# Clustered attention and a softplus layer on one core: weight steps with one VectorE operation fewer, an upright first pass, keys 4 to 7 held back, a shorter softplus

## The chip, the cores and the metric

The kernel runs on one core of one Trainium2 chip. Such a core has five engines that run side by side and meet at semaphores: TensorE (PE, matrix products; its weight loads are listed as PEld), VectorE (DVE), ScalarE (ACT), GpSimd (POOL) and SyncE (SP, which here only issues transfers). Each takes its instructions in the order in which they were written for it. Sixteen DMA engines carry the transfers that SP and ACT issue. Products accumulate in PSUM, everything else lies in SBUF.

The metric is the device time of one execution in microseconds; before the change it is 899.57 us, the median of three runs.

## What is computed

Attention of 4 batches with 8 heads over 768 positions of 64 numbers, in which a query sees only the keys of its own cluster, and then a layer with softplus. Cut to what matters:

```python
q_n, k_n, c_n = (x / (norm(x) + 1e-6) for x in (q, k, centroids))   # 16 centroids a head
q_assign = argmax(einsum('bhsd,hcd->bhsc', q_n, c_n), -1)           # and k_assign likewise
mask   = q_assign[:, :, :, None] == k_assign[:, :, None, :]
scores = where(mask, q @ k.T / 8, -1e9)
attn   = exp(scores - max(scores)); attn = attn / (sum(attn) + 1e-9)
x = concat_heads(attn @ v)                                          # 3072 x 512
h = x @ w_in                                                        # 512 -> 2048
g = maximum(h, 0) + log1p(exp(-abs(h)))                             # softplus
out = g @ w_out                                                     # 2048 -> 512
```

The inputs are drawn at random with fixed spreads. The two weight matrices come in as 64-bit floats, the rest as 32-bit floats.

## The kernel before

**Numbers in two halves.** A 32-bit value is carried as two f16 tiles, a rounded one and the rest. A product is then three f16 products (rounded x rounded, and the two mixed ones). The rest is always made on POOL by subtraction (lines 336, 372, 457, 641, 719, 795), after ACT made the rounded half (lines 335, 368, 455, 639, 717, 794).

**Passes.** A pass is half of one batch's query positions: 8 passes, each with 8 heads and 3 query tiles of 128 positions, 24 tiles. Tile `t` of pass 0 is `t < 24`; pass 0 and 1 belong to batch 0.

**Preparation.** `prep_k` loads two heads' keys, splits them, transposes them, lets `nearest` find each key's centroid (small products with `cents`, then a row of small DVE operations), and writes into the second tile `n2` of each key its rounded numbers and, beside them, 16 columns that hold 0 for its own cluster and a large negative number for the others. `prep_q` does the same for four heads' queries and waits for the clusters that have a key at all (`al`, made in `clusters`). So a score with its mask is a sum of two products over 128 rows (lines 574 to 582). `turn` transposes either on PE through PSUM (keys 0 to 7 and the queries of pass 0) or by a DMA transpose in SP's queue (`flip`). `prep_v` loads and splits the values. `prep_weights` has 32 steps, 16 for `w_in` and 16 for `w_out`: a step loads 512 KB of 64-bit floats into a staging room (most rooms are parts of the tile `wo` itself), and rebuilds a 32-bit float from the two words: ACT takes the magnitude of the high word, scaled down so far that the exponent is rebased (line 320), DVE shifts it left by three bits (322), joins the sign bit of the high word (326) and joins three bits of the low word (332). ACT and POOL then make the two f16 halves (335, 336).

**Scores and attend.** For each tile `scores` makes four 384-wide matmuls (line 576) into one of two PSUM banks pairs of the ring `s`, DVE takes the negated maximum of each row (592), ACT the exponential with it as bias (600). From pass 1 on, ACT and POOL split the result (639, 641) and a DMA transpose turns two tiles at once (650) for `attend`, which multiplies by the values (683 to 685; a column of ones gives the sum of the weights). In pass 0 this is done in 32 bits instead: ACT also accumulates the sum (`accum_out`), PE transposes the weights (617, six of 128x128, against a 32-bit unit matrix `eye32`), ACT and DVE copy them out of PSUM (625, 623), and `attend` multiplies with the unsplit values (679). Lines 702 to 710 divide by the sums.

**The layer.** `ffn1` makes 16 tiles of `h` in each pass (752 to 754), `softplus` turns each into two halves of `g`: DVE sets the sign bit (771), ACT takes Exp and Ln(1 + .) (773, 774), DVE adds max(h, 0) (783), then the split (794, 795). `ffn2` sums over 16 of these (817 to 819) into the one PSUM bank of the ring `o`, in two halves of 8, for three output tiles; `store` scales and adds (833, 837) and SP writes the result (840).

**Order.** No engine decides what it does next. When the program is built, the class `Order` runs every piece of work as a generator that yields operations with an engine and an assumed time in ns, and waits on events and on rings of buffers (`ring`). It always emits the operation that can start first by these assumed times; a priority breaks ties only. Operations marked `shared` are planned so that DVE and POOL do not overlap. So an assumed time, a wait or an engine that changes in one place changes the written order of all engines. All loads are issued in ACT's queue (line 221), transposes and stores in SP's. Where the plan leaves PE idle for more than 600 ns, `warm` (line 204) writes small filler matmuls.

Of the kernel before, what the change touches and what calls it, by code (L numbers as in the profile page):

```python
# [17 lines left out]
MASK = 65504.0  # L18
# [7 lines left out]
NPE = 8  # L26

REBASE = 2.0**-112

# [84 lines left out]
def tile_cluster_attention__then__softplus_ffn(  # L114
# [47 lines left out]
    cf = cpool.tile([P, D], F32, name="cf")  # L162
    nc.sync.dma_start(cf, centroids.rearrange("h c d -> (h c) d"))
    tab = cpool.tile([P, 2 * NT, NCL], F16, name="tab")
# [9 lines left out]
    eye32 = p2.tile([P, P], F32, tag="ot", name="eye32", bufs=QT)  # L174
    nc.gpsimd.tensor_copy(eye32, eye)
# [10 lines left out]
    for i in range(2):  # L186
        t = cpool.tile([P, 2 * NT, P], F16, name=f"n2_{i}")
        nc.gpsimd.memset(t[:, :, D + NCL :], 0.0)
        N2.append(t)


    od = Order()

    eye32_key = od.get("ot", QT)[1]
# [25 lines left out]
    def load(dst, src, nbytes):  # L220
        return op("ACT", 60, lambda: nc.scalar.dma_start(dst, src), dma=nbytes / 290.0)
# [10 lines left out]
    def prep_centroids():  # L232
        sq = p2.tile([P, D], F32, tag="x32", name="csq", bufs=1)
# [53 lines left out]
    def prep_weights(step: int):  # L287
# [30 lines left out]
        if f >= 0 and f // 2 in rooms:  # L318
            yield wait("wr", rooms[f // 2])
        yield op("ACT", 630, lambda: nc.scalar.activation(mag, val, AF.Abs, scale=sc))  # L320
# [5 lines left out]
            lambda: nc.vector.scalar_tensor_tensor(high, high, -0x80000000, mab, ALU.bitwise_and, ALU.bitwise_or),  # L326
# [31 lines left out]
    def prep_v(n: int):  # L358

        vk = yield from ring("vb", NP)  # L360
        rk, vf = yield from raw_tile("v", n, [P, 2, NT, D])
        yield load(vf, rows(v, n, 0, NT, 2), P * 2 * NT * D * 4)
        vb = VB[n // 2 % NP]
        raw_v[n] = vf, rk
# [17 lines left out]
    def turn(dst, src, name: str, on_chip: bool):  # L382
# [4 lines left out]
        for g in range(0, dst.shape[1], NT):  # L387
# [8 lines left out]
            if g:  # L396
                yield op("DVE", 950, lambda g=g, ps=ps: nc.vector.tensor_copy(dst[:, g : g + NT], ps))
# [6 lines left out]
    def nearest(xs, heads, low: int, sfx: str, twin: int):  # L404
# [28 lines left out]
        yield op("DVE", 345, lambda: nc.vector.tensor_tensor(sim, sim, tab[:, :nt], ALU.mult))  # L433
# [10 lines left out]
    def prep_k(n: int):  # L444

        kkey[n // 2] = yield from ring("kt", NP)
        rk, kf = yield from raw_tile("k", n, [P, 2, NT, D])
# [27 lines left out]
            250,  # L475
# [8 lines left out]
    def clusters(n, ps, eq, hk):  # L484
# [4 lines left out]
        if h % 4 == 0:  # L489
            alive[n] = p2.tile([P, 4, NCL], F16, tag="al", name=f"al_{n}", bufs=4)  # L490
# [5 lines left out]
        yield op("DVE", 150, lambda: nc.vector.tensor_scalar(al, al, 1.0, None, ALU.min), shared=True)  # L496
        od.set(("al", n))

    def prep_q(n: int, pi: int):
# [4 lines left out]
        yield wait("kn", n + 2)  # L504
# [56 lines left out]
    def scores(t: int):  # L561
# [5 lines left out]
        if t:  # L567
            yield wait("sc", t - 1)
# [346 lines left out]
```

## Time and profile before

| | |
|---|---|
| three runs | 896.24, 899.57 and 903.73 us |
| span of the profiled execution | 899.4 us |
| mean granted clock of TensorE | 0.992 |
| moved by DMA | 136.12 MB, mean 151 GB/s |
| first score matmul | 53.1 us from the start |
| last score matmul of the last pass | 779.6 us |

The profile is of one execution. Its span runs from the first to the last instruction, and is 0.2 us below the median of the runs. Instructions of an engine are grouped by their line in the kernel; a group's row has the engine, the operation, the tiles that it writes and reads, the count, and behind the bar the busy time in us and the mean of one in ns, then the idle time of the engine in front of them with what ended it.

The page's strip of 40 slices of 22.5 us each shows where PE is not full (tenths of a slice) and how that lies against the other engines and the transfers:

```profile
PE   7889998989889999999999999999999999999997
...
DVE  4989997778876656765757666657675655433331
ACT  5667686866757677865858777766787576633330
POOL 5322356787857678866757677675777665512110
PEclk8999999999999999999999999999999999999999
DMA  6323759988896879999696989997888655510000
```

DVE is at nine tenths in the second to sixth slice, POOL fills only from the sixth on, and DMA is at nine tenths of its 16 engines in many slices from the eighth on. PE's strip contains the filler of line 204.

### The profile page before, as it was taken

Reading aid. Unit: us, or ns where it says so; the run is one execution under the profiler, and the core shown is the slowest. Engines: PE = TensorE matmul, PEld = TensorE weight load, DVE = VectorE, ACT = ScalarE, POOL = GpSimd, SP = SyncE. Lnnn points to the kernel's source line nnn. Section 1 sums busy time; section 2 is a strip of 40 time slices with the busy share of each in tenths; the row PEclk is TensorE's granted clock in tenths of the full one; section 3 lists DMA queues with packets and bytes.
Section 4 is the critical chain, followed back from the end, with each engine's and each line's share of the span. In section 5 each row is a group of like instructions: output and inputs, shape, how many; then the busy total and the mean of one; then the engine's idle time right before and its main releaser. Section 6 shows DMA issues by size and latency. Waiting matters only on the chain.

```text
span 899.4 us, 20880 instructions
## 1 busy us (share of the span) xinstructions
PE 859.1 (96%) x8650; PEld 562.1 (62%) x8650; DVE 576.5 (64%) x1060; ACT 588.2 (65%) x904; POOL 528.1 (59%) x353
## 2 busy tenths in 40 slices
PE   7889998989889999999999999999999999999997
PEld 7878876655565666655666665555666565655554
DVE  4989997778876656765757666657675655433331
ACT  5667686866757677865858777766787576633330
POOL 5322356787857678866757677675777665512110
PEclk8999999999999999999999999999999999999999
DMA  6323759988896879999696989997888655510000
GB/s 202 117 89 112 154 150 214 202 194 212 168 190 150 189 151 191 226 201 210 149 198 126 187 166 193 195 220 135 182 182 186 145 119 134 111 30 12 25 0 36
DMA packets 393326, 136.12 MB, mean 151 GB/s; under 512 B 369680, under 2 KB 386064, under 8 KB 393232
## 3 DMA queue, kind: packets, MB, share of 16 engines
q1 hardware_dynamic: 371472, 99.15, 56.2%
q10 hardware_dynamic: 21760, 35.66, 13.4%
q8 instruction: 67, 1.10, 0.5%
q14 instruction: 27, 0.22, 0.1%
HBM read 35.68 MB, written 6.29 MB: 47 GB/s over the span
## 4 chain that ended last, share of the span: by engine, by line
PE 73%; DVE 8%; DMA 8%; ACT 4%; issue 3%; POOL 3%; ACTq 1%; POOLq 0%; DVEq 0%
PE s L576 10%; PE o L817 8%; PE o L819 8%; PE o L818 8%; PE h L752 8%; PE h L754 8%; PE h L753 8%; DMA pt<-phl 8%; PE mbank L679 3%; PE mbank L683 3%; PE mbank L685 3%; PE mbank L684 3%; POOL phl L641 2%; PE pT L617 2%; DVE negm L592 2%
## 5 line engine op out<-in xcount | busy, mean ns | idle before, releaser
L641 POOL TENSOR_TENSOR phl<-p,phl 128x768 f16<-128x768 f32 x168 | 278.3, 1672 | 84.8 <-ACT phl L639 61.2
L592 DVE TENSOR_REDUCE negm<-s 128x1 f32<-128x768 f32 x192 | 182.6, 954 | 51.5 <-PE s L576 48.0
L600 ACT ACTIVATE p<-s,negm 128x768 f32<-128x768 f32 x192 | 172.1, 898 | 65.6 <-DVE negm L592 45.5
L795 POOL TENSOR_TENSOR gh<-fg,gh 128x768 f16<-128x768 f32 x64 | 107.2, 1676 | 135.2 <-ACT gh L794 131.8
L752 PE MATMUL h<-xT,wi 128*128 128x384 f16 x512 | 167.4, 327 | 7.4 <-DVE fg L783 5.4
L754 PE MATMUL h<-xT,wi 128*128 128x384 f16 x512 | 167.8, 328 | 0.0
L753 PE MATMUL h<-xT,wi 128*128 128x384 f16 x512 | 167.6, 327 | 0.0
L576 PE MATMUL s<-kt,qt 128*128 128x384 f16 x768 | 155.5, 325 | 3.7 <-ACT p L600 3.3
L819 PE MATMUL o<-wo,gh 128*128 128x512 f16 x384 | 145.8, 380 | 1.1 <-POOL gh L795 1.1
L817 PE MATMUL o<-wo,gh 128*128 128x512 f16 x384 | 146.0, 380 | 0.7 <-DVE ot L837 0.4
L818 PE MATMUL o<-wo,gh 128*128 128x512 f16 x384 | 145.9, 380 | 0.0
L773 ACT ACTIVATE fa<-fa 128x384 f32<-128x384 f32 x128 | 66.6, 521 | 120.1 <-DVE fa L771 119.2
L639 ACT CAST phl<-p 128x768 f16<-128x768 f32 x168 | 134.3, 827 | 16.3 <-DMA pt<-phl 14.1
L771 DVE TENSOR_SCALAR fa<-h 128x384 int32<-128x384 int32 x128 | 71.0, 555 | 107.7 <-PE h L754 107.4
L683 PE MATMUL mbank<-vb,pt 128*128 128x65 f16 x1008 | 108.5, 192 | 8.2 <-DMA pt<-phl 7.8
L684 PE MATMUL mbank<-vb,pt 128*128 128x64 f16 x1008 | 108.5, 192 | 0.0
L685 PE MATMUL mbank<-vb,pt 128*128 128x65 f16 x1008 | 108.2, 194 | 0.0
L683 PEld LDWEIGHTS <-pt 128*128 128x128 f16 x1008 | 93.4, 98 | 22.9 <-DMA pt<-phl 11.4
L783 DVE SCALAR_TENSOR_TENSOR fg<-h,fa 128x384 f32<-128x384 f32 x128 | 70.5, 552 | 53.5 <-ACT fa L774 51.6
L576 PEld LDWEIGHTS <-qt 128*128 128x128 f16 x768 | 71.6, 98 | 49.4 <-issue 6.2
L684 PEld LDWEIGHTS <-pt 128*128 128x128 f16 x1008 | 92.9, 97 | 11.1
L685 PEld LDWEIGHTS <-pt 128*128 128x128 f16 x1008 | 93.1, 97 | 0.0
(122 smaller groups left out, 1289.9 us busy)
## 6 DMA issues: line engine op xcount, KB each, us to landing
wo<-in_moe_w_in_dram ACTq DMA_DIRECT2D x16, 512.0 KB, 3.7
wo<-in_moe_w_out_dram ACTq DMA_DIRECT2D x14, 512.0 KB, 4.0
rawk<-in_k_dram ACTq DMA_DIRECT2D x16, 384.0 KB, 4.7
rawv<-in_v_dram ACTq DMA_DIRECT2D x16, 384.0 KB, 4.6
rawq<-in_q_dram ACTq DMA_DIRECT2D x16, 384.0 KB, 4.1
out_dram<-ot SPq DMA_DIRECT2D x24, 256.0 KB, 2.6
pt<-phl SPq DMA_TRANSPOSE x84, 5.7
wraw<-in_moe_w_out_dram ACTq DMA_DIRECT2D x2, 512.0 KB, 5.3
```

The source lines that it names most:

```text
L576: nc.tensor.matmul(st[:, j, :SH], qt[:, s, i], kt[:, s, NT // 2 * j : NT // 2 * (j + 1)], start=(s == 0), stop=(s == 1),)
L592: yield op("DVE", 950, lambda: nc.vector.tensor_reduce(negm, st[:, :, :SH], AX.XY, ALU.max, negate=True))
L641: "POOL", 1640, lambda: nc.gpsimd.tensor_tensor(phl[:, u, 1], p32, phl[:, u, 0], ALU.subtract), shared=True
L683: nc.tensor.matmul(av, pt[:, 0, c], vb[:, c, D : 2 * D + 1], start=(c == 0), stop=False)
L684: nc.tensor.matmul(av[:, :D], pt[:, 0, c], vb[:, c, :D], start=False, stop=False)
L685: nc.tensor.matmul(av, pt[:, 1, c], vb[:, c, D : 2 * D + 1], start=False, stop=(c == NT - 1))
L752: nc.tensor.matmul(hp, w[0], x[0], start=(c == 0), stop=False)
L753: nc.tensor.matmul(hp, w[0], x[1], start=False, stop=False)
L754: nc.tensor.matmul(hp, w[1], x[0], start=False, stop=(c == NP - 1))
L817: nc.tensor.matmul(po, g[0], wo[:, f, 0, 0], start=(f == f0), stop=False)
L818: nc.tensor.matmul(po, g[0], wo[:, f, 0, 1], start=False, stop=False)
L819: nc.tensor.matmul(po, g[1], wo[:, f, 0, 0], start=False, stop=(f == f0 + NF // 2 - 1))
```

## The change

- **Weight steps.** Line 320 uses the activation Prelu with a slope of 2^32 for negative numbers instead of the magnitude. A negative number then lands 32 exponent steps higher, which after the shift by three is a set sign bit. The join of the sign (line 326) is gone, and line 332 joins the low word's bits to the shifted word.
- **Loads.** All loads are issued by SP instead of ACT, with an assumed 450 ns instead of 60.
- **Upright first pass.** In pass 0 the scores are made with the keys as rows, so that no transpose of the weights is needed. Two 384-wide matmuls on the second product alone (rounded numbers and mask, 96 of the rows) give an estimate of each query's maximum; DVE negates it and splits it into a coarse and a fine part (two operations on 128x1), PE transposes these, ACT writes them into two rows of the transposed queries, 96 and 97, against constant rows of 2048 and 1 in the keys. Twelve 128-wide matmuls then make the shifted scores upright, and ACT takes the exponential straight into the tile that `attend` reads. `eye32`, the 32-bit transposes, their copies and `accum_out` are gone. A column of ones behind the values of pass 0 gives the sums; these values are loaded in two parts, into rows of 65 numbers. Both `m` and `u`, the two score tiles, come from the ring `s`.
- **Keys 4 to 7.** `prep_k` of heads 4 and 6 waits, in the planner, until the first queries' cluster work is through (`qa`); the first queries no longer wait for the second keys' buffer.
- **Softplus.** g = max(h, min(ln(1 + exp h), 20)): Exp reads PSUM directly, line 771 is gone, line 783 becomes one operation with minimum and maximum.
- **Last half.** The last pass's second half of `ffn2` takes its PSUM from the ring `s`, two tiles, instead of the one of `o`.
- **Assumed times and small things.** A DVE copy in `turn` 560 instead of 950, two small DVE operations 450 and 300 instead of 250 and 150. `tab` is one row, read by broadcast.

```diff
@@ prep_weights
-        yield op("ACT", 630, lambda: nc.scalar.activation(mag, val, AF.Abs, scale=sc))
+        yield op("ACT", 630, lambda: nc.scalar.activation(mag, val, AF.Prelu, scale=sc, alpha=SIGN_UP))
         yield op("DVE", 420, lambda: nc.vector.tensor_scalar(mab, mab, 3, None, ALU.logical_shift_left), shared=True)
         yield op(
             "DVE",
             680,
-            lambda: nc.vector.scalar_tensor_tensor(high, high, -0x80000000, mab, ALU.bitwise_and, ALU.bitwise_or),
-            shared=True,
-        )
-        yield op(
-            "DVE",
-            680,
-            lambda: nc.vector.scalar_tensor_tensor(high, low, 29, high, ALU.logical_shift_right, ALU.bitwise_or),
+            lambda: nc.vector.scalar_tensor_tensor(high, low, 29, mab, ALU.logical_shift_right, ALU.bitwise_or),
             shared=True,
         )
@@ load
-        return op("ACT", 60, lambda: nc.scalar.dma_start(dst, src), dma=nbytes / 290.0)
+        return op("SP", 450, lambda: nc.sync.dma_start(dst, src), dma=nbytes / 290.0)
@@ prep_v
-        rk, vf = yield from raw_tile("v", n, [P, 2, NT, D])
-        yield load(vf, rows(v, n, 0, NT, 2), P * 2 * NT * D * 4)
+        rk, vf1 = yield from raw_tile("v", n, [P, 2, NT, D + (n < H)])
+        vf = vf1[:, :, :, :D]
+        if n < H:
+            yield op("POOL", 150, lambda: nc.gpsimd.memset(vf1[:, :, :, D:], 1.0))
+        parts = 2 if n < H else 1
+        for u in range(0, 2, 2 // parts):
+            yield load(
+                vf[:, u : u + 2 // parts], rows(v, n + u, 0, NT, 2 // parts), P * 2 * NT * D * 4 // parts
+            )
@@ prep_k
         kkey[n // 2] = yield from ring("kt", NP)
+        if n in (4, 6):
+            yield wait("qa", 0)
@@ prep_q
-        yield wait("kn", n + 2)
+        yield wait("kn", n + 2 if n else 0)
@@ upright, for each tile of pass 0
+        def emit():
+            for j in range(2):
+                nc.tensor.matmul(
+                    st[:, j, :SH],
+                    qt[:SHIFT, 1, i],
+                    kt[:SHIFT, 1, NT // 2 * j : NT // 2 * (j + 1)],
+                    start=True,
+                    stop=True,
+                )
+        yield op("PE", 330, emit)
...
+        yield op("DVE", 950, lambda: nc.vector.tensor_reduce(negm, st[:, :, :SH], AX.XY, ALU.max, negate=True))
+        od.set(sk)
...
+        yield op("DVE", 90, lambda: nc.vector.tensor_scalar(top, negm, 1.0 / by, None, ALU.mult))
+        yield op("DVE", 90, lambda: nc.vector.scalar_tensor_tensor(rest, top, -by, negm, ALU.mult, ALU.add))
...
+        yield op("PE", 60, lambda: nc.tensor.transpose(out=ps[:KROWS], in_=mc, identity=eye))
+        yield op("ACT", 250, lambda: nc.scalar.copy(qt[SHIFT:KROWS, 1, i], ps[SHIFT:KROWS]))
...
+        def emit():
+            for c in range(NT):
+                to = up[:, c // (NT // 2), c % (NT // 2) * P : (c % (NT // 2) + 1) * P]
+                nc.tensor.matmul(to, kt[:, 0, c], qt[:, 0, i], start=True, stop=False)
+                nc.tensor.matmul(to, kt[:KROWS, 1, c], qt[:KROWS, 1, i], start=False, stop=True)
+        yield op("PE", 690, emit)
...
+        yield op("ACT", 830, lambda: nc.scalar.activation(dst, up[:, :, :SH], AF.Exp))
@@ scores, pass 0
-                for c in range(NT // 2):
-                        nc.tensor.transpose(out=ps[:, c], in_=p32[:, j, c * P : (c + 1) * P], identity=eye32)
...
-                    yield op("DVE", 550, lambda: nc.vector.tensor_copy(dst, ps))
-                else:
-                    yield op("ACT", 490, lambda: nc.scalar.copy(dst, ps))
+        if pi == 0:
+            yield from upright(t)
+            return
@@ softplus
-            lambda: nc.vector.tensor_scalar(a.bitcast(I32), hp.bitcast(I32), -0x80000000, None, ALU.bitwise_or),
-        yield op("ACT", 520, lambda: nc.scalar.activation(a, a, AF.Exp))
+        yield op("ACT", 500, lambda: nc.scalar.activation(a, hp, AF.Exp))
         yield op("ACT", 520, lambda: nc.scalar.activation(a, a, AF.Ln, bias=1.0))
-            "DVE", 550, lambda: nc.vector.scalar_tensor_tensor(g[:, f % 2], hp, 0.0, a, ALU.max, ALU.add)
+            "DVE", 550, lambda: nc.vector.scalar_tensor_tensor(g[:, f % 2], a, TOP, hp, ALU.min, ALU.max)
@@ ffn2
+        if pi == len(passes) - 1 and half:
+            ok = yield from ring("s", 2)
+            po = ps_s.tile([P, 2, DM], F32, tag="s", name=f"o_{b}_{c0 + i}_{half}")[:, 0]
+        else:
+            ok = yield from ring("o", 1)
+            po = ps_o.tile([P, DM], F32, tag="o", name=f"o_{b}_{c0 + i}_{half}")
```

More of the change, by code (lines that the diff above doesn't have):

```diff
@@ L188, in tile_cluster_attention__then__softplus_ffn @@
         nc.gpsimd.memset(t[:, :, D + NCL :], 0.0)
+        for c, m in zip(range(SHIFT, KROWS), SHIFT_BY):
+            nc.gpsimd.memset(t[:, :, c : c + 1], m)
         N2.append(t)
+    MC = []
+    for i in range(2):
+        t = cpool.tile([P, KROWS], F16, name=f"mc_{i}")
+        nc.gpsimd.memset(t, 0.0)
+        MC.append(t)
     od = Order()
-    eye32_key = od.get("ot", QT)[1]
     mbank = ps_m.tile([P, 512], F32, name="mbank")
@@ L232, in prep_centroids @@
     def prep_centroids():
-        sq = p2.tile([P, D], F32, tag="x32", name="csq", bufs=1)
+        sq = cfs[:, 1]
         small = [cpool.tile([P, 1], F32, name=f"c{nm}") for nm in ("ss", "sg", "nrm", "rn")]
@@ L488, in clusters @@
         yield op("PE", 100, lambda: nc.tensor.matmul(cnt, ones, eq, start=True, stop=True))
-        if h % 4 == 0:
-            alive[n] = p2.tile([P, 4, NCL], F16, tag="al", name=f"al_{n}", bufs=4)
+        if n - h % 4 not in alive:
+            alive[n - h % 4] = p2.tile([P, 4, NCL], F16, tag="al", name=f"al_{n}", bufs=4)
         al = alive[n - h % 4][:, h % 4 : h % 4 + 2]
@@ L567, in scores @@
         if t:
-            yield wait("sc", t - 1)
+            yield wait("scm" if tiles[t - 1][1] == 0 else "sc", t - 1)
+        if pi == 0:
+            yield from upright(t)
+            return
         sk = yield from ring("s", 2)
@@ L594, in scores @@
         p32 = p2.tile([P, 2, SH], F32, tag="p32", name=f"p32_{sfx}", bufs=3)
[L595 to L631 removed]
+        yield op("ACT", 900, lambda: nc.scalar.activation(p32, st[:, :, :SH], AF.Exp, bias=negm))
+        od.set(sk)
         if u == 0:
@@ L678, in emit @@
                 for c in range(NT):
[L679 removed]
+                    nc.tensor.matmul(av, pt[:, c], vf[:, c], start=(c == 0), stop=(c == NT - 1))
                 return
@@ L803, in ffn2 @@
         yield wait("g", pi, NF // 4 * half)
-        ok = yield from ring("o", 1)
-        po = ps_o.tile([P, DM], F32, tag="o", name=f"o_{b}_{c0 + i}_{half}")
+        if pi == len(passes) - 1 and half:
+            ok = yield from ring("s", 2)
+            po = ps_s.tile([P, 2, DM], F32, tag="s", name=f"o_{b}_{c0 + i}_{half}")[:, 0]
+        else:
+            ok = yield from ring("o", 1)
+            po = ps_o.tile([P, DM], F32, tag="o", name=f"o_{b}_{c0 + i}_{half}")
         f0 = NF // 2 * half
```

106 lines of the change are left out of this document (58 added, 48 removed).

## The prediction

> **What bounds the kernel now.** I read the page's head, then the windows view cut at the places where the work changes, then the same windows for line 204 alone, then the grouped instructions and the waits. In the windows view each row is a stretch, its length, and the busy us (and instructions) of PE, PEld, DVE, ACT and POOL, then the granted clock, the DMA share and GB/s.
>
> ```profile
> span 899.4 us, 20880 instructions
> ...
> 0.00:53.20 53.20, 42.83 (x731) 40.77 (x732) 38.48 (x114) 28.73 (x41) 22.75 (x23) 0.94 0.48 155
> 53.20:126.00 72.80, 70.94 (x657) 63.21 (x655) 67.11 (x112) 53.44 (x107) 22.72 (x19) 1.00 0.47 118
> 126.00:140.00 14.00, 11.83 (x172) 9.61 (x172) 12.98 (x22) 10.79 (x16) 8.72 (x7) 1.00 0.88 211
> 140.00:280.00 140.00, 122.45 (x1397) 82.04 (x1395) 106.78 (x184) 97.31 (x150) 100.85 (x67) 0.98 0.92 194
> 280.00:876.00 596.00, 592.77 (x5554) 356.08 (x5555) 347.97 (x625) 396.03 (x591) 371.43 (x239) 1.00 0.72 148
> ```
>
> The same stretches for line 204 alone. Its matmuls are filler that the planner puts into gaps, so they are idle time in disguise.
>
> ```profile
> 0.00:53.20 53.20, 30.27 (x435) 28.01 (x435) 0.94 0.48 155
> 53.20:126.00 72.80, 6.64 (x111) 6.28 (x111) 1.00 0.47 118
> 126.00:280.00 154.00, 25.58 (x422) 23.95 (x422) 0.98 0.91 196
> ```
>
> From 280 to 876 PE is busy 592.8 of 596.0 us: nothing but less PE work shortens that. Real PE work (busy less filler) is 12.6 of 53.2 us before the first scores, 64.3 of 72.8 in pass 0, and 108.7 of 154.0 from 126 to 280. So 40.6 + 8.5 + 45.3 = 94 us stand empty before 280, and a little at the end; all that can be won lies there. Within pass 0 the fullest engine beside PE is DVE, 67.1 of 72.8 us. From 126 to 280 none is full: DVE 119.8 of 154.0, POOL 109.6, DMA share 0.91.
>
> **The parts, and what each costs.** The groups that the change touches (busy us and mean ns of one):
>
> ```profile
> L326 DVE SCALAR_TENSOR_TENSOR wo<-wo 128x512 int32<-128x512 int32 x14 | 14.9, 1066 | 0.0
> L326 DVE SCALAR_TENSOR_TENSOR wraw<-wraw,wo 128x512 int32<-128x512 int32 x2 | 1.4, 680 | 0.0
> L623 DVE COPY ptf<-pT 128x384 f32<-128x384 f32 x24 | 13.1, 552 | 0.7 <-PE pT L617 0.2
> L702 DVE TENSOR_SCALAR rs<-mbank 128x6 f32<-128x6 f32 x28 | 4.5, 162 | 13.3 <-PE mbank L685 13.2
> L702 DVE TENSOR_SCALAR rs<-sum 128x6 f32<-128x6 f32 x4 | 2.4, 602 | 0.0
> L625 ACT COPY ptf<-pT 128x384 f32<-128x384 f32 x24 | 11.3, 477 | 5.1 <-PE pT L617 4.7
> L600 ACT ACTIVATION_READ_ACCUMULATOR p<-s,negm 128x1 f32 x24 | 4.7, 195 | 0.0
> ...
> 0.00:53.20 53.20, 4.41 (x5) 0.94 0.48 155
> 53.20:126.00 72.80, 12.28 (x14) 1.00 0.47 118
> 126.00:280.00 154.00, 14.06 (x13) 0.98 0.91 196
> ...
> 126.00:280.00 154.00, 12.15 (x22) 0.98 0.91 196
> ```
>
> The last four rows are windows: DVE time of line 326 in three stretches, then of line 771.
>
> *Weight steps.* Line 326 goes, 19 times before 126. As measured that is 4.41 + 12.28 = 16.7 us of DVE. But an undisturbed one takes 680 ns, and the 1066 of the others is the same operation kept waiting. I count only 0.68, so 19 x 0.68 = 12.9 us. The Trainium skill (GPSIMD Engine Reference, Specifications) says that GpSimd shares its SBUF interfaces with VectorE, and that this hurts DVE instructions with two SBUF inputs or in a two-port mode. By that rule the wait passes to the next such operation and 12.9 us is right; without it the whole 16.7 would go. The spread of 680 to 1066 agrees with the rule.
>
> *Upright pass 0, DVE.* 24 copies of line 623 go: 13.1 us. 48 tiny operations on 128x1 come in. No row is that small; the nearest is line 702 with 128x6, 162 ns from PSUM and 602 from SBUF. 48 x 0.162 = 7.8 us, 48 x 0.602 = 28.9 us. The new ones read SBUF, but POOL, whose work goes with the long ones, is busy only 22.7 of 72.8 us here: 0.162 + 0.31 x 0.44 = 0.30 each, so 14.4 us. Line 702 reads PSUM alone in the changed kernel, four times; that is too little to count. DVE's work until 126 falls by 12.9 + 13.1 - 14.4 = 11.6 us (18.2 with tiny operations at 162 ns, 2.9 more than before at 602).
>
> *Upright pass 0, PE and ACT.*
>
> ```profile
> 60.44 0.66 PE pT L617 x6
> 61.10 1.30 PE s L576 x8
> ...
> 63.06 1.29 PE mbank L679 x12
> ...
> 52.95 0.28 PE qT L393 x5
> ```
>
> A tile now takes 0.65 (four 384-wide score matmuls) + 0.66 (six transposes) + 1.29 us. Changed: 0.33 for the two matmuls of the maximum, about 0.1 for one small transpose, and twelve 128-wide matmuls. These take 0.65 us by columns (0.163 x 128/384 x 12) and 0.98 by the worst nearby row, qT at 0.08 each with its waits; I take 0.68, since they follow each other like the scores. That is 1.11 for 1.31, 5 us less over 24 tiles (between -6 and +2). One more column in line 679 adds 1.29/64, or 0.5 us over pass 0. ACT loses 11.3 + 4.7 us and gains 24 small copies, at most L625's 0.48 each. Both are covered by DVE, which paces the stage.
>
> *Keys 4 to 7 held.* Nothing is removed; two key chains move from before the first scores into pass 0, so scores start well before 53.2. The wait is one of the planner, so no engine stands at it; only the written order changes. I count nothing for it: pass 0 is paced by DVE, whose sum is the same. It is what lets the 11.6 us come out at the end of pass 0. Otherwise PE, with 64.3 - 5 us of work after a start at 53.2, would be next. The cover is the 12 tiles before head 4, some 36 us at 72.8/24; if a chain is late by more, PE waits a few us.
>
> *Loads on SP.* All 80 loads move behind the DMA transposes of SP's queue.
>
> ```profile
> L221 ACTq DMA_DIRECT2D wo<-in_moe_w_out_dram x14: 333/336/486, 105.0 to 245.1; - x14
> 6.50 0.20 ACT L244 ACTIVATE cnrm<-csg 128x1 f32<-128x1 f32 x1 [4.48 <-issue]
> wo<-in_moe_w_out_dram ACTq DMA_DIRECT2D x14, 512.0 KB, 4.0
> ...
> 7.74 1.64 POOL L457 TENSOR_TENSOR kn<-rawk,kn 128x768 f16<-128x768 f32 x1 [5.05 <-ACT kn L455]
> ```
>
> ACT gets back 0.34 us for each, hidden beside PE. At the start the centroids' Ln waits 4.48 us behind the engine's own issues; freed, it moves up by some 2.5 us, and the centroid transposes that PE has in front of the first key's move too. I take 2 us (0 to 2.5). The values' loads are split into rows of 256 bytes and so slower, covered because values are not needed until the first attend. POOL's few new memsets at the start (columns of the value tiles, of N2, the MC tiles) fall into the 5.05 us in which it waits for its first key, up to 7.74; behind that they would cost their own length.
>
> *Shorter softplus.* Line 771 goes, 128 times. 106 of them lie after 280, beside a full PE, and are worth nothing. In the ramp the two removals take 22 x 0.55 = 12.2 us and 14.1 us from DVE. PE's idle time there, by the waits:
>
> ```profile
> PE mbank L683 <- DMA pt<-phl: 5.6, 4, 3.3
> PE h L752 <- DVE fg L783: 5.4, 4, 4.1
> PE mbank L204 <- DVE x L710: 3.3, 2, 1.8
> ```
>
> The DVE-bound ones are 5.4 + 3.3 = 8.7 us, the filler stands for more. Between 0 (DMA sets the ramp) and the whole 26.2 us, I take 7, near the waits that name DVE.
>
> *Second output bank in the last half.*
>
> ```profile
> 883.30 0.23 PE o L819
> 883.56 0.70 DVE ot L837
> 884.30 0.38 PE o L817
> ...
> 877.51 0.56 DVE L771 TENSOR_SCALAR fa<-h 128x384 int32<-128x384 int32 x1 [2.21 <-PE h L754]
> ```
>
> Between two output tiles PE waits from 883.36, when the last matmul's slot ends, to 884.30: 0.94 us, twice, gone with two banks. The last softplus chain before them is shorter by line 771's 0.56. Together 2.4 us.
>
> The corrected due times (250 to 450, 950 to 560) change only the written order; no row prices that, and it is left at nothing.
>
> **Sum.** 899.4 - 11.6 - 2 - 7 - 2.4 = 876.4. The profiled execution's 899.4 is within 0.2 us of the median 899.57, so the sum stands for the median too.
>
> **Rivals.**
> *The ramp closes (about 850).* The tiny operations cost 162 ns, so DVE loses 18 us in pass 0, and all 26.2 us of the ramp come out: 899.4 - 18.2 - 2 - 26.2 - 2.4 = 850.6. For it: DVE at 119.8 of 154. Against: POOL and DMA are as full.
>
> *Loads delay transposes (about 892).* The chain between 126 and 280 has four long waits on a transpose:
>
> ```profile
> 144.08 11.40 DMA pt<-phl
> ...
> 247.58 9.26 DMA pt<-phl
> ...
> 261.11 6.08 DMA pt<-phl
> ...
> 273.09 6.79 DMA pt<-phl
> ```
>
> A weight load takes 4.0 us to land. If one lies ahead in the same queue each time, 4 x 4.0 = 16 us come back: 892. The Trainium skill (DMA: Bandwidth & Descriptors, Issuing engines are not separate DMA queues) holds that all DMAs run on the same 16 engines, so the move would change only who spends the issue time. By that page this rival is wrong; this trace cannot show it, having no plain load in SP's queue beside transposes.
>
> *Pass 0 keeps its length (888.0).* Each tile now needs a score bank twice. The holds are 0.33 + 0.95 and 0.68 + 0.90 us, 2.86 over two banks, or 1.43 a tile against a pace of 3.03. Only waits of 1.6 us in each hold would make it the bound. Then the 11.6 is lost: 888.0.
>
> *SP stands still (slower, about 911).* A weight load waits in SP for its staging room, which POOL's line 336 frees, and the transposes behind it stand too. In the ramp that operation itself waits 28.3 us over 9:
>
> ```profile
> POOL wo L336 <- ACT wo L335: 28.3, 9, 4.9
> ```
>
> 3.1 us for each of 16 w_out loads is 50 us; were 35 to reach PE, the time is 911. It decides from 32.2 us in all, which is 2 us a load: then it is over 908.6. Against it: the planner orders SP by due times, a load among them.
>
> **Numbers.** Forecast 0.58, the ramp closing 0.11, delayed transposes 0.14, pass 0 unchanged 0.08, SP standing still 0.09. About 1% (9 us) is what a measurement can tell here. Under 890.6 lie nearly all of the forecast, the first rival, some of the second and half of the third: faster 0.77; slower is most of the last, 0.08; the rest, 0.15, is the same. The range leaves out about half of the 850 case below and the 911 case with the upper edge of 892 above: 855 to 897. The forecast's own range is 860 to 890.
>
> **What would show it.** First scores before 45 us and the last score of pass 0 some 15 us earlier, with DVE still the fullest engine there: the first term. No line-204 filler between the last output tiles: the tail. An unchanged stretch of full PE of some 600 us: the bound. It is wrong if SP's waits on weight rooms or the transposes' landing grow, or if PE in pass 0 waits on score banks.

## The result, and the profile after

The changed kernel takes 867.07 us (median of four runs, 866.7 to 870.9). The kernel before took 900.79 us on the same chip, so the ratio is 0.965, with a 95% interval of 0.960 to 0.970. The profiled execution spans 865.5 us, 33.9 us less than before. The forecast was 876.4 us with a range of 855 to 897: right in its direction and its range, 9 us too high, and, as the experiments show, wrong in most of its reasons. One execution of a later kernel (late weight steps) took 2245 us and is left out of the median given for it.

The head and the strip of the page after:

```profile
span 865.5 us, 20493 instructions
...
PE   7799899999999999999999999999999999999997
...
DVE  6887866666657545655655646667554534321211
...
DMA  9623759999899999998969999999898767610000
```

PE is at nine tenths from the sixth slice to the last but one, where before it fell back to eight in slices 7, 9, 11 and 12. DVE, at nine tenths before in the second and in the fourth to sixth slice (the third has eight), is nowhere above eight. DMA is at nine tenths in most slices from the seventh to the thirtieth. Now the windows view, cut at the first score matmul (36.6 us), and behind it the same view for the filler alone, which is line 214 here. Columns are as in the prediction.

```profile
0.00:36.60 36.60, 27.77 (x472) 26.46 (x473) 28.02 (x81) 20.15 (x30) 18.79 (x29) 0.95 0.89 282
36.60:126.00 89.40, 82.96 (x1024) 75.26 (x1022) 69.52 (x165) 64.76 (x110) 37.11 (x30) 0.98 0.42 111
126.00:140.00 14.00, 11.11 (x164) 8.73 (x162) 10.43 (x15) 11.81 (x17) 10.69 (x7) 1.00 1.12 216
140.00:280.00 140.00, 136.05 (x1510) 87.77 (x1509) 91.21 (x168) 104.66 (x158) 104.78 (x71) 1.00 1.05 203
280.00:842.00 562.00, 561.82 (x5252) 337.79 (x5249) 278.30 (x493) 371.02 (x564) 350.54 (x226) 1.00 0.80 149
...
0.00:36.60 36.60, 20.26 (x322) 19.18 (x322) 0.95 0.89 282
36.60:126.00 89.40, 12.98 (x202) 11.60 (x199) 0.98 0.42 111
126.00:280.00 154.00, 16.04 (x259) 14.73 (x259) 1.00 1.06 204
```

Length less busy time plus filler is what PE stands empty. Until 126 that is 126.0 - 110.7 + 33.2 = 48.5 us, where before it was 40.6 + 8.5 = 49.1. From 126 to 280 it is 154.0 - 147.2 + 16.0 = 22.9, where before it was 45.3. So the first scores come 16.5 us earlier, and yet next to nothing is won by 126 us: the last attend matmul of pass 0 starts at 125.6, before at 126.9. The gain lies in the ramp, as the stretch from 126 to 280 is called: 22.4 us of it. The other 11.5 are the first 126 us (0.6), the stretch from 300 to 840, where PE stands empty for 0.2 us instead of 4.1 (3.9), the tail behind 840 (2.3), and less PE work (4.7, the effect of the granted clock included). They are worked out in the same way, from windows of PE and of the filler; PE's work is its busy time over the whole execution less the filler, 790.7 us before and 786.0 after.

What changed in the ramp is seen in the POOL subtraction that ends a weight step (line 336 before, 340 after), in windows before and after 126 us. The first two rows are of before, the others of after:

```profile
0.00:126.00 126.00, 21.74 (x18) 0.97 0.47 134
126.00:300.00 174.00, 16.36 (x14) 0.98 0.89 192
...
0.00:126.00 126.00, 29.52 (x25) 0.97 0.56 161
126.00:300.00 174.00, 8.13 (x7) 1.00 1.06 202
```

Of 32 weight steps 18 were done by 126 us before, and 25 are now. The ramp has 7 of them to carry instead of 14, and the last one starts at 225.7 instead of 277.5 us. Each step left out of the ramp takes a 512 KB load, two ACT and two or three DVE operations and 1.2 us of POOL out of a stretch in which DVE, POOL and DMA were well filled and none was full.

The next view lists a line's instructions: shortest, median and longest issue in ns, then the start of the first and of the last. The first row is the load of `w_in` before, the other two are `w_in` and `w_out` after:

```profile
L221 ACTq DMA_DIRECT2D wo<-in_moe_w_in_dram x16: 334/335/1157, 5.3 to 101.1; - x16
...
L231 SPq DMA_DIRECT2D wo<-in_moe_w_in_dram x16: 327/385/2217, 5.7 to 50.6; - x16
L231 SPq DMA_DIRECT2D wo<-in_moe_w_out_dram x14: 328/506/1877, 72.4 to 181.9; - x14
```

All of `w_in` is on its way by 50.6 us instead of 101.1. That the earlier loads are what makes the earlier steps is a guess so far; the experiments test it.

### The profile page after: what moved, and what is told of

It is laid out like the page before. It is cut to its first block, busy times and chain, and to the rows that moved or that the text cites. A ratio compares the mean times of both kernels' runs of the same rounds, so it can differ in the third digit from the quotient of the medians.

```text
span 865.5 us, 20493 instructions
## 1 busy us (share of the span) xinstructions
PE 838.4 (97%) x8539; PEld 546.1 (63%) x8539; DVE 480.7 (56%) x924; ACT 575.3 (66%) x880; POOL 524.0 (61%) x362
## 4 chain that ended last, share of the span: by engine, by line
PE 67%; issue 10%; POOL 4%; ACT 2%; DVE 2%; DMA 1%; POOLq 0%; ACTq 0%; DVEq 0%
PE s L661 11%; PE o L865 7%; PE o L867 7%; PE o L866 7%; PE h L801 7%; PE h L803 7%; PE h L802 7%; PE mbank L733 3%; PE mbank L735 3%; PE mbank L734 3%; POOL gh L839 2%; POOL phl L691 1%; DMA pt<-phl 1%; ACT p L680 1%; DVE negm L677 1%
## 5 line engine op out<-in xcount | busy, mean ns | idle before, releaser
L677 DVE TENSOR_REDUCE negm<-s 128x1 f32<-128x768 f32 x168 | 160.2, 956 | 98.6 <-PE s L661 96.5
L680 ACT ACTIVATE p<-s,negm 128x768 f32<-128x768 f32 x168 | 150.7, 899 | 55.4 <-DVE negm L677 37.9
L817 ACT ACTIVATE fa<-h 128x384 f32<-128x384 f32 x128 | 62.4, 490 | 127.3 <-PE h L803 126.8
L827 DVE SCALAR_TENSOR_TENSOR fg<-fa,h 128x384 f32<-128x384 f32 x128 | 70.4, 550 | 133.1 <-ACT fa L818 132.6
L661 PE MATMUL s<-kt,qt 128*128 128x384 f16 (+1 forms) x672 | 136.0, 325 | 2.8 <-ACT p L680 2.3
L661 PEld LDWEIGHTS <-qt 128*128 128x128 f16 (+1 forms) x672 | 62.7, 98 | 45.0 <-issue 3.4
L803 PEld LDWEIGHTS <-wi 128*128 128x128 f16 x512 | 49.8, 97 | 33.4
```

The costliest lines, as they stand in the source:

```text
L661: nc.tensor.matmul(st[:, j, :SH], qt[:rows, s, i], kt[:rows, s, NT // 2 * j : NT // 2 * (j + 1)], start=(s == 0), stop=(s == 1),)
L677: yield op("DVE", 950, lambda: nc.vector.tensor_reduce(negm, st[:, :, :SH], AX.XY, ALU.max, negate=True))
L803: nc.tensor.matmul(hp, w[1], x[0], start=False, stop=(c == NP - 1))
```

## The experiments

Twelve kernels ran. The table gives, beside the times, the weight steps done by 126 us (from the windows of the subtraction above) and how long PE stands empty in two stretches, worked out as above. Ratios are to the kernel before on the same chip; profiled spans are those of one execution.

| kernel | median us | ratio, 95% interval | span | steps by 126 | PE empty to 126 | 126 to 300 |
|---|---|---|---|---|---|---|
| before | 900.79 | - | 899.4 | 18 | 49.1 | 45.3 |
| after | 867.07 | 0.965 (0.960 to 0.970) | 865.5 | 25 | 48.5 | 22.9 |
| old weight steps | 884.95 | 0.984 (0.979 to 0.988) | 882.4 | 20 | 51.1 | 32.6 |
| old softplus | 874.13 | 0.971 (0.967 to 0.976) | 868.7 | 25 | 48.7 | 25.6 |
| loads on ACT | 901.70 | 1.002 (0.999 to 1.005) | 895.3 | 17 | 50.6 | 47.3 |
| keys not held | 872.76 | 0.970 (0.966 to 0.974) | 871.1 | 25 | 54.4 | 22.4 |
| weight loads on ACT | 893.60 | 0.995 (0.991 to 0.998) | 890.7 | 20 | 52.7 | 43.2 |
| q, k, v loads on ACT | 879.90 | 0.978 (0.975 to 0.981) | 877.6 | 24 | 56.2 | 25.5 |
| loads on ACT, written earlier | 910.48 | 1.011 (1.006 to 1.016) | 910.0 | 21 | 63.1 | 27.0 |
| late weight steps | 882.76 | 0.982 (0.978 to 0.985) | 880.6 | 18 | 49.6 | 37.1 |
| old pass 0 | 882.95 | 0.981 (0.977 to 0.984) | 881.1 | 26 | 53.7 | 27.9 |
| loads on SP alone | 889.42 | 0.988 (0.984 to 0.992) | 886.7 | 20 | 53.9 | 32.8 |
| weight steps after the first queries | 867.28 | 0.964 (0.960 to 0.968) | 865.9 | 23 | 48.3 | 25.0 |
| the same, loads free | 871.12 | 0.967 (0.963 to 0.971) | 865.1 | 25 | 50.7 | 20.4 |

Of the 20 steps of loads on SP alone, the last is still under way at 126 us. Every edit also makes the planner write a new order for all engines. What a new order is worth by itself was not measured, so a difference of a few us between two kernels is weak evidence.

**Undoing one part each.** The first is the weight step with its old join of the sign.

```diff
-        yield op("ACT", 630, lambda: nc.scalar.activation(mag, val, AF.Prelu, scale=sc, alpha=SIGN_UP))
+        yield op("ACT", 630, lambda: nc.scalar.activation(mag, val, AF.Abs, scale=sc))
...
+            lambda: nc.vector.scalar_tensor_tensor(high, high, -0x80000000, mab, ALU.bitwise_and, ALU.bitwise_or),
```

> The changed kernel with the weight steps as before (magnitude on ACT, sign joined by DVE's third operation). Theory 1: the changed kernel won some 23 us between 126 and 280 because 25 of its 32 weight steps end on POOL before 126 (18 before the change), and it is the DVE time of the sign join that paid for them. Then fewer steps, about 20, end before 126, the emptiness of PE between 126 and 300 grows from 22 us to over 30, and the time is 877 to 885. Rival 2 (the shorter softplus won the ramp) and rival 3 (loads off ACT's queue won it): 867 to 872, and 24 or 25 steps still end before 126.

Its steps in the two windows:

```profile
0.00:126.00 126.00, 23.77 (x20) 0.99 0.51 150
```

It has 20 steps by 126, PE stands empty in its ramp for 9.7 us longer than in after, and the time is 884.95. Its last attend of pass 0 starts at 125.5, where after has 125.6. So the DVE operation that was removed is not paid out at the end of pass 0; five more steps fit before it. Count, ramp and time all lie where the first theory had them; 7.2 of the 16.9 us that the span grows by lie outside the ramp.

The second undoing is the softplus.

```diff
+            lambda: nc.vector.tensor_scalar(a.bitcast(I32), hp.bitcast(I32), -0x80000000, None, ALU.bitwise_or),
-        yield op("ACT", 500, lambda: nc.scalar.activation(a, hp, AF.Exp))
+        yield op("ACT", 520, lambda: nc.scalar.activation(a, a, AF.Exp))
-        lambda: nc.vector.scalar_tensor_tensor(g[:, f % 2], a, TOP, hp, ALU.min, ALU.max)
+        lambda: nc.vector.scalar_tensor_tensor(g[:, f % 2], hp, 0.0, a, ALU.max, ALU.add)
```

> The changed kernel with the softplus as before (DVE sets the sign bit first). Rival 2: DVE's 22 sign operations in the ramp, 12 us, and the longer hold of the h banks bring back 8 to 14 us: 875 to 881. Theory 1 and rival 3: 0 to 4 us, 867 to 871, of which 0.6 in the last chain.

The profile is 3.2 us longer, of which 2.7 lie between 126 and 300; the median of the runs is 7 us longer with a wide spread (870.93 to 877.25), over which the granted clock falls from 0.996 to 0.986. Steps and their times stay. It lies between the theories: the 12 us of DVE that it puts back into the ramp cost 3 to 7, so this DVE work is a small part of the 22.4.

The third puts the loads back into ACT's queue.

```diff
-        return op("SP", 450, lambda: nc.sync.dma_start(dst, src), dma=nbytes / 290.0)
+        return op("ACT", 60, lambda: nc.scalar.dma_start(dst, src), dma=nbytes / 290.0)
```

> The changed kernel with all loads issued by ACT again. Rival 3: weight loads then wait in ACT's queue behind its own work, steps slip behind 126 as before the change, and 10 to 20 us come back: 877 to 887. Theory 1 and rival 2: ACT is not the pace, 865 to 871, and 24 or 25 steps end before 126.

Here every range was missed: the whole gain is gone, though less DVE work, the upright pass 0 and the short softplus are all still there. Rival 3 had the direction, and its size was 15 us too small. Its steps in the two windows, and its loads:

```profile
0.00:126.00 126.00, 19.68 (x17) 0.96 0.46 127
126.00:300.00 174.00, 17.31 (x15) 0.98 0.98 195
...
L231 ACTq DMA_DIRECT2D wo<-in_moe_w_in_dram x16: 334/341/647, 1.8 to 100.6; - x16
```

17 steps by 126, one less than before the change, and `w_in` goes out until 100.6 as it did before. The ninth and tenth loads show why, in the timelines of ACT in this kernel and of SP and ACT in after:

```profile
59.06 0.34 ACTq L231 DMA_DIRECT2D wo<-in_moe_w_in_dram  x1
64.27 0.81 ACT L637 ACTIVATE ptf<-u 128x768 f32<-128x768 f32 x1 [2.24 <-PE u L619]
64.87 0.33 ACTq L231 DMA_DIRECT2D wo<-in_moe_w_in_dram  x1
66.08 0.67 ACT L330 ACTIVATE wi<-wo 128x512 f32<-128x512 f32 x1
```

```profile
13.77 4.92 SPq L231 DMA_DIRECT2D wo<-in_moe_w_in_dram  x5
...
21.21 29.70 SPq L231 DMA_DIRECT2D wo<-in_moe_w_in_dram  x9
48.07 0.69 ACT L330 ACTIVATE wi<-wo 128x512 f32<-128x512 f32 x1
```

In ACT's queue a load stands behind computations: the ninth goes out at 59.06 for a use at 66.08, and the tenth, at 64.87, stands behind line 637, which had waited 2.24 us for PE. SP has nothing to compute: it issues five weight loads in a row from 13.77 and nine more over the 29.7 us from 21.21, so the ninth is issued at 22.5 and used at 48.07. Over steps 1 to 15 the mean time from issue to use is 19.1 us in after, 6.3 here and 5.1 in the kernel before. What SP pays for this is small. The waits of SP in the whole execution of after, and then that of PE in its ramp for transposed weights, each with its sum in us, its count and its longest:

```profile
SPq L231 <- POOL wi L340: 26.4, 9, 6.7
...
SPq L231 <- POOL wo L340: 12.1, 3, 5.5
```

```profile
PE mbank L733 <- DMA pt<-phl: 1.5, 2, 0.9
```

SP stands 26.4 + 12.1 = 38.5 us with a load in front of a weight room, 12 times, just as the rival feared, but PE's waits in the ramp for a transposed tile come to 1.5 us, where the kernel before had 5.6. SP reaches a room early and waits for it; the waits lie ahead of need.

The fourth drops the hold of the keys.

```diff
-        if n in (4, 6):
-            yield wait("qa", 0)
...
-        yield wait("kn", n + 2 if n else 0)
+        yield wait("kn", n + 2)
```

> The changed kernel without the hold: keys 4 to 7 are not held, the first queries wait for the second keys' buffer. First score matmuls at 45 to 52 us instead of 36.6. Theory 1: pass 0 ends at the same place (last attend of pass 0 within 3 us of 125.6), because the order spends what is free on weight steps in either case; 865 to 870. Rival 4 (the early first scores are what let weight steps pass early): the end of pass 0 moves by 5 us or more and the time is 873 or more.

The first score matmul moves from 36.6 to 52.5 us and the last attend of pass 0 only from 125.6 to 126.1, as expected, but the time is 5.7 us longer, between the two ranges. Until 126 PE stands empty for 54.4 us instead of 48.5. So the earlier start that the hold gives does not shorten pass 0, but more of PE's other work is done by its end.

**Which loads, and why.** A fifth theory was formed from these: the queue counts because SP runs ahead of the plan. Two kernels divide the loads.

```diff
+    def load(dst, src, nbytes, sp=True):
+        if not sp:
+            return op("ACT", 60, lambda: nc.scalar.dma_start(dst, src), dma=nbytes / 290.0)
```

with `sp=False` at the weight loads in one kernel, at the loads of q, k and v in the other.

> The changed kernel with the 32 weight loads alone issued by ACT; keys, queries and values stay on SP. Theory 5 (running ahead): in SP's queue the weight loads leave as soon as a staging room is free, 20 us and more before their use, while in ACT's queue each stands in its written place among ACT's work, 6 us ahead of its use, so a step takes the length of a load and the steps slip past 126. Then nearly everything comes back: 890 to 902, 16 to 19 steps done by 126. Rival 6 (ACT's issue time, or the start of the keys and queries, is what counts): 867 to 878.

> The changed kernel with keys', queries' and values' loads on ACT, the weight loads on SP. Theory 5: 866 to 873, weight steps as in the changed kernel. Rival 6: 880 to 900.

With the weights alone on ACT the time is 893.60, inside what the theory asked; the steps by 126 are 20, one above it. The mean lead of the loads falls to 5.6 us. So 26.5 us of the gain hang on 32 instructions of 0.34 us each standing in one queue or the other, and on the order that the plan writes around them. With q, k and v alone on ACT the time is 879.90, missed by 7 us, with the edge of rival six just not reached. The steps are almost all there (24), but the start is late. Its ACT timeline at the start:

```profile
0.77 0.98 ACTq L232 DMA_DIRECT2D rawk<-in_k_dram  x2
1.78 12.09 ACTq L232 DMA_DIRECT2D rawv<-in_v_dram  x4
```

Four value loads take 12.09 us to issue, 3.0 each, and the centroids' and keys' ACT work stands behind them. The first scores come at 44.5 us instead of 36.6, and pass 0 ends 5.8 us later. That is a second, different reason for SP: not when a load goes, but what stands behind its issue.

The next kernel leaves all loads on ACT and lets the plan write them earlier.

```diff
+        od.set(("wl", step))
         yield load(raw64, src[:, c, e * WC : (e + 1) * WC], P * WC * 8)
-        od.set(("wl", step))
```

> All loads on ACT, but in the plan a weight load may be issued once the one before is issued, where it waited for its landing. Theory 5: loads are written further ahead in ACT's queue, the lead over their use grows beyond 10 us for steps 2 to 15, and at least half of the 34 us returns: 868 to 884. Rival 6: ACT's issue time stays, so the time stays at 893 or more.

Theory 5 missed by 26 us: 910.48 lies where the rival had it. The lead did grow, to 14.5 us, and 21 steps are done by 126. But the price shows in the waits of ACT (the head of the cores view ahead of it) and in the first 126 us:

```profile
core 0: 910.0 us, clock 0.971
...
ACT cnrm L254 <- DMA wo<-in_moe_w_in_dram: 12.0, 1, 12.0
...
0.00:126.00 126.00, 100.94 (x1243) 94.74 (x1244) 81.04 (x205) 66.85 (x110) 46.75 (x51) 0.82 0.45 142
```

ACT stands 12.0 us in issuing before its first computation, the first scores come at 49.5 us, and PE is granted 0.82 of its clock until 126. The last attend of pass 0 starts only at 152.2, so what the table has from 126 to 300 is not the same work here. An early load on a computing engine was paid by that engine. Whether loads on ACT could be early without that cost was not tried.

**Are the weight steps the cause, or only a sign?** One kernel keeps every part of the change and only holds steps 18 to 31, in the planner, until pass 0 is attended. So its count of steps by 126 is that of before.

```diff
+        if step >= 18:
+            yield wait("at", H * QT - 1)
```

> The changed kernel with weight steps 18 to 31 held back in the plan until pass 0 is attended, so that 18 steps are done by about 126, as in the kernel before. Theory 1: the ramp then has 14 steps again and PE's emptiness from 126 to 300 grows by 10 to 20 us, while pass 0 ends 3 to 8 us earlier: 872 to 885. Rival 7 (it does not matter when the steps run, what counts is that they are shorter and their loads are there): 863 to 870.

```profile
0.00:126.00 126.00, 21.48 (x18) 0.97 0.46 132
126.00:300.00 174.00, 16.25 (x14) 0.98 1.05 205
```

Pass 0's last attend starts 5.1 us earlier, at 120.5, and the ramp is 37.1 us empty instead of 22.9; the time is 882.76. Seven steps more in the ramp cost 14.2 us there, 2.0 each, as the first theory had it. But the hold stands in front of the load, so 14 loads were held with their steps, and ACT waited for them in the ramp, which it hardly did in after (0.5 us in the whole execution):

```profile
ACT wo L332 <- DMA wo<-in_moe_w_out_dram: 8.0, 4, 5.1
```

How much of the 14.2 is the steps and how much is their late loads was not separated. Nor is the count all that matters. With 12 steps left PE stands empty in the ramp for 32.6 us (old weight steps) and 32.8 (loads on SP alone), but for 43.2 with the weight loads on ACT; with 14 left it is 37.1 here and 45.3 in the kernel before, whose loads are on ACT. So at an equal count the ramp is some 8 to 11 us emptier where ACT issues the weight loads. Why was not tested.

**The remaining parts.** The next gives pass 0 its old form, scores as rows and 32-bit transposes (line 617 and the copies of the old listing), in the changed kernel; the one after puts loads on SP into the kernel before and changes nothing else.

```diff
-        if pi == 0:
-            yield from upright(t)
-            return
+        if pi == 0:
...
+                        nc.tensor.transpose(out=ps[:, c], in_=p32[:, j, c * P : (c + 1) * P], identity=eye32)
```

> The changed kernel with pass 0's scores, transposes and copies as before the change. By the prediction's terms PE gets 5 us more work in pass 0 and DVE 3 to 9 us more (13.1 less the measured 10.8 of the tiny operations and what they wait). Theory 1: the DVE part costs weight steps, 22 to 24 done by 126, and together 874 to 882. Rival 9 (pass 0 has slack, its end is set by other things): 865 to 871.

> The kernel before with its loads on SP and nothing else. Theory 5: the weight loads run ahead by themselves, the lead of steps 1 to 15 grows from 5 to over 12 us, 20 to 22 steps are done by 126 and the time is 880 to 893. Rival 8 (the parts work only together: without the DVE time that the sign join gave back the loads only lie and wait): 894 to 902.

The old pass 0 gives 882.95, near the time expected but for another reason. Steps by 126 are 26, not 22 to 24. Its span is 15.6 us longer: PE work is 5.0 us more than in after (a clock of 0.990 for 0.996 included), and PE stands empty 5.2 us more until 126 and 5.0 more in the ramp, with a pass 0 that ends at 132.9, 7.3 us later. So the upright pass earns by an earlier end of pass 0 and perhaps by PE's work, and not by more weight steps.

Loads on SP alone bring 889.42, a ratio of 0.988: about 11 of the 34 us. Steps rise from 18 to 20 and the lead of the loads from 5.1 to 18.6 us.

```profile
L221 SPq DMA_DIRECT2D wo<-in_moe_w_in_dram x16: 327/328/1712, 6.2 to 62.6; - x16
```

So the parts need each other. Without the loads on SP the rest of the change is worth nothing (901.70); without the rest the loads are worth 11; together they are worth 34. The counts fit a simple reading: a step that has its data early can use free DVE time, and free DVE time is of no use to a step whose data are late.

**Trying to do better.** With everything in place the first scores could start still earlier if the weight steps gave way to them. One kernel holds the work of each step but the first, not its load, until the first queries' clusters are done; another also lets the next load go as soon as the last is issued.

```diff
+        if step:
+            yield wait("qa", 0)
         yield op("ACT", 630, lambda: nc.scalar.activation(mag, val, AF.Prelu, scale=sc, alpha=SIGN_UP))
```

> The changed kernel with the work of weight steps 1 and up held, in the plan, until the first queries' cluster work is through; their loads still go out. By theories 1 and 5 nothing is lost on the steps, since their loads lie ready, and the first queries no longer share DVE and ACT with them: first score matmuls at 30 to 35 us instead of 36.6, 858 to 866. Rival 10 (the steps lost at the start are missing in the ramp): 868 to 875.

> As the last one, and in the plan a weight load may be issued once the one before is issued instead of landed. On SP that costs no engine, so leads grow again: 856 to 866 by theory 5; 867 or more if the loads then stand in front of keys and queries in SP's queue at the start.

Neither beats the change: 867.28 lies between the two ranges, 871.12 in that of loads in front of keys and queries. In the first, scores start at 32.1 and the last attend of pass 0 at 117.4 us, 8.2 earlier, but two steps fewer are done by 126. PE's empty time until 126 is 48.3 us against 48.5, and from 126 to 300 it is 25.0 against 22.9. Work was only exchanged. No version that ran is clearly faster than the changed kernel.

The corrected assumed times and the second output bank were not run by themselves. The bank is seen in the trace, below. One more edit is in the kernel and not in the list of the change: from pass 1 on, the second score product runs over 96 rows instead of 128 (line 661). In after a matmul of either kind takes 325 ns, so no time of a matmul is won by it.

## Why the prediction was right or wrong, step by step

**The bound.** Right. From 280 to 842 PE is busy 561.8 of 562.0 us, and all of the gain but the PE work itself and 3.9 us lies outside the stretch that was full.

**11.6 us less DVE in pass 0, to "come out at the end of pass 0".** This step failed. DVE's busy time until 126 did fall, from 105.6 to 97.5 us, with seven more steps in it. But the last attend of pass 0 starts 1.3 us earlier, not 11.6, and its last score matmul, which was to come some 15 us earlier, starts at 122.5 instead of 118.8. The failing sentence is "pass 0 is paced by DVE, whose sum is the same". Its 67.1 of 72.8 us had weight steps in it that the order had filled in. With the scores started at 36.6, DVE is busy 69.5 of 89.4 us: still the fullest beside PE (70.0 without the filler), as the prediction's sign asked, but with 19.9 us to spare, so its sum does not set the length. The DVE time that the sign join gave back went to steps, as the old weight step (20 steps against 25) shows. What ends pass 0 at 125.6 with no engine full stays open; steps held back move it by 5.1 and 8.2 us, so the steps written in between are part of it.

The size of the small DVE operations, priced at 0.30 us each between 0.162 and 0.602, was near. Here are their groups in after, with those of the join that is left (line 336), and behind them two groups of before, the join that is left (332 there) and the one that was removed (326):

```profile
L602 DVE TENSOR_SCALAR mc<-negm 128x1 f16<-128x1 f32 x24 | 3.4, 152 | 0.5 <-PE mT L606 0.2
L603 DVE SCALAR_TENSOR_TENSOR mc<-mc,negm 128x1 f16<-128x1 f16 x24 | 7.4, 320 | 0.2
L336 DVE SCALAR_TENSOR_TENSOR wo<-wo,wi 128x512 int32<-128x512 int32 x16 | 12.2, 771 | 0.1
L336 DVE SCALAR_TENSOR_TENSOR wo<-wo 128x512 int32<-128x512 int32 x14 | 10.4, 750 | 0.3
...
L332 DVE SCALAR_TENSOR_TENSOR wo<-wo 128x512 int32<-128x512 int32 x30 | 24.4, 813 | 0.0
L326 DVE SCALAR_TENSOR_TENSOR wo<-wo,wi 128x512 int32<-128x512 int32 x16 | 14.5, 905 | 0.2
```

They took 3.4 + 7.4 = 10.8 us in place of 14.4. The prediction left out the 16 joins of `w_in`, at 905 ns, which are most of the 19 before 126; its 1066 is that of `w_out`. The wait that was said to pass to the next two-input operation is not seen there: the join that is left took 771 and 750 ns, where it had taken 813 before. So the sum of 16.7 us was nearer for the join than 12.9. The rule of the Trainium skill (GPSIMD Engine Reference, Specifications) that was weighed there is neither refuted nor shown by it, since POOL's overlap with it changed too. The twelve upright matmuls that start at 72.29 us take 0.70 us to the next operation's start; 0.68 was forecast.

**5 us less PE work in pass 0, "covered by DVE".** The cover was wrong and the size stays open. PE's work fell from 790.7 to 786.0 us, by 4.7, and what fell came off the span, because PE's empty time until 126 stayed (49.1 and 48.5 us). But the kernel before with its loads on SP alone, which has the same matmuls as before, has 857.28 - 72.61 = 784.7 us of it at a clock of 0.997, where before has 0.992 and after 0.996. So two executions of the same matmuls, at different granted clocks, differ by as much, and neither the 4.7 nor the 5.0 that the old pass 0 puts back (at 0.990) can be put down to the upright matmuls.

**2 us at the start.** The mechanism was right, its worth was not. The centroids' Ln runs at 3.13 us instead of 6.50, and the first key's transposes at 8.31 instead of 12.74. But PE's empty time until 126 fell by 0.6 us only.

**The hold of the keys, at nothing.** First scores before 45 us was right (36.6). But without the hold the kernel takes 5.7 us more, with the same end of pass 0; the hold earns its part by PE's empty time (54.4 against 48.5), and is not "what lets the 11.6 us come out".

**Loads on SP, priced as 0.34 us of ACT each and hidden.** This is the large miss. It took the place of the issuing instruction for the whole of the effect. The trace of before allowed another reading: the last `w_in` load goes out at 101.1 us, in a queue that waits for PE, with its use close behind it. The sum had a price only for what the move costs (two rivals), and none for loads that go earlier. By the runs the move is worth 11 us alone and 35 with the rest (901.70 less 867.07). The Trainium skill (DMA: Bandwidth & Descriptors, Issuing engines are not separate DMA queues) holds that all DMAs run on the same 16 engines whichever engine issues them, and that issuing from several saves issue time alone. As to what loads take from transposes the runs agree: the transposes' median landing is 6.2 us with the loads in their queue and 6.5 with the loads on ACT. As to the time they do not: what the queue decides here is when a load is issued.

**7 us in the ramp from less DVE.** Right in place, and a third of the size: 22.4 us. The prediction took the same 14 weight steps to be in the ramp and made each cheaper. Half of them left it instead, which with their loads is 14.2 by the late weight steps. Of the other 8 the softplus is 2.7 by its profile. The rest goes, as far as the runs show, with the queue of the loads rather than with DVE work: loads on SP alone brings the ramp from 45.3 to 32.8 with two steps fewer in it and all the DVE work of before.

**2.4 us in the tail.** Right: 2.3 by the emptiness of PE behind 840 us. The timeline of after between the last output tiles:

```profile
851.18 0.38 PE L865 MATMUL o<-wo,gh 128*128 128x512 f16 x1
...
851.38 0.69 DVE L885 SCALAR_TENSOR_TENSOR ot<-o,ot 128x512 f32<-128x512 f32 x1 [3.77 <-PE o L867]
```

PE begins the next output tile at 851.18 while DVE reads the last one from 851.38 on; before, it stood for 0.94 us there.

**The rivals.** That loads delay transposes, and that SP stands still, fell: SP did stand, without harm. The closing of the ramp, given 0.11 and 850 us, was nearest to what happened in its place (a ramp of 22.9 us empty in place of 45.3), though not by its reason. That pass 0 keeps its length came true in its result, a pass 0 that ends where it did, but it was not a loss, since the time was spent on weight steps. The forecast came near because its misses had both signs: of the first two terms 11.6 + 2 - 0.6 = 13.0 us did not come, and 0.1 of the tail, while 15.4 more in the ramp, 3.9 between 300 and 840 and 4.7 of PE work came uncounted. That is 10.9 us more than forecast, the difference of 876.4 and the span of 865.5. That the time fell into the range is luck in good part.

## What to carry to other kernels

Where a queue is in order, a load in a computing engine's queue goes out when that engine gets to it; so compare each load's issue with its first use, and give the issuing to an engine with nothing to compute if the lead is only the landing time. An engine that looks like the pace of a stage may only be full of work that a planner has put there from elsewhere: ask what would flow into its free time, and look for the gain where that work came from. When parts of a change are needed by each other, price them together too; here undoing five parts one at a time cost 29.8 + 16.9 + 15.6 + 5.6 + 3.2 = 71 us of span in sum, of a gain of 34.

## What was not expected of the hardware

The time to issue one transfer is not a constant. This is the list of the value loads in the kernel with q, k and v on ACT, shortest, median and longest issue in ns:

```profile
L232 ACTq DMA_DIRECT2D rawv<-in_v_dram x20: 374/411/3514, 1.8 to 603.3; - x20
```

The first four, while SP issued eight weight loads beside them, took 12.09 us together, where the median one takes 0.41; and the engine's next computation stood behind them. The kernel with all loads on ACT has the same four loads with no load of SP beside them but that of the centroids:

```profile
2.29 5.63 ACTq L231 DMA_DIRECT2D rawv<-in_v_dram  x4
```

They take 5.63 us, 1.4 each. So they are long by themselves at the start, and twice as long beside SP's loads. Why they are longer than the median was not tried.

The granted clock of TensorE fell to 0.82 over the first 126 us of the kernel whose loads were written earlier on ACT, against 0.97 in after, and its PE work came to 798.5 us instead of 786.0. Its start is late and broken up; that this is the reason was not tested.

In these runs the transposes are not slower for sharing a queue with plain loads. The 84 transposes of `pt` have a median landing of 6.2 us, against 6.5 in the changed kernel with all loads on ACT; and of 5.0 in the kernel before with its loads on SP, against 5.7 with them on ACT. The loads of `w_in` took 6.4 us to land instead of 3.7, which their lead of 19.1 us covers.
